# First half of the keys loaded as float32 through ScalarE's hardware queue, and cast on VectorE

## Chip, cores, metric

One core of a Trainium2 chip. The metric is the device time of one execution in microseconds (us). Most executions of a kernel agree within 0.3%, some 0.7 us here. In the views PE is TensorE, PEld its weight loads, DVE VectorE, ACT ScalarE, POOL GpSimd and SP SyncE. A hardware queue here is one that ScalarE or SyncE issues transfers on.

## The reference

Attention over 32 memory slots per head, then a bilinear feed-forward layer. The inputs are float32, the output is 4608 x 512 float32.

```python
# q, k, v: (8 batches, 8 heads, 576, 64); phi: (8, 8, 576, 32)
a = softmax(phi, axis=2)                      # over the sequence
k_m = einsum('bhsm,bhsd->bhmd', a, k)         # 32 keys per head
v_m = einsum('bhsm,bhsd->bhmd', a, v)
attn = softmax(q @ k_m.T / 8, axis=-1) @ v_m
x = attn -> (4608, 512)
out = ((x @ w_a) * (x @ w_b)) @ w_out         # w_a, w_b: 512x1536, w_out: 1536x512
```

## The kernel before

The kernel works in float16. Transfers issued by GpSimd cast from float32 on the way. phi alone stays float32 in SBUF, as ScalarE reads it for the exponential. All loads of the first two batches and all weights are issued ahead, in this order:

```python
kv_sbs = [consts.tile([P, 3, NHP, NI * D], F16, name=f"kv_sb{t}") for t in range(2)]

def load_phi(b):
    phis[b] = inp.tile([P, NHP, NI * M], F32, name="phi_sb")
    (nc.sync if b == 0 else nc.gpsimd).dma_start(out=phis[b], in_=rows(phi, b))

def load_k(b, hps=slice(0, NHP)):
    kvs[b] = kv_sbs[b % 2]
    nc.gpsimd.dma_start(out=kvs[b][:, 0, hps], in_=rows(k, b)[:, hps])
# ... load_v, load_q, load_wab (wa_sb and wb_sb), load_wo alike, on gpsimd

nc.scalar.preload_act_table_set("natural_log_exp_and_others")
load_phi(0)
halves = [slice(0, 2), slice(2, 4)]
for x in halves:
    load_k(0, x)
    load_q(0, x)
load_v(0)

warm = consts.tile([P, 512], F16, name="warm")
nc.vector.memset(warm, 0.0)
# ...
make_identity(nc, ident)
for t in range(2):
    nc.vector.memset(kv_sbs[t][:, 2], 1.0 / CS)      # the two masks
load_wab(0, 256)
# ... ones: a memset on vector, two affine_selects on gpsimd
load_wab(256, 512)
load_wab(512, 1024)
load_wab(1024, 1536)
load_wo(0)
load_phi(1)
load_k(1)
load_q(1, halves[0])
load_wo(1)
load_q(1, halves[1])
for x in halves:
    load_v(1, x)
load_wo(2)
```

The third plane of `kv_sb` is a constant mask; it makes the key sums (`ks`) also give the sum of the exponentials. The reciprocal of that sum and the scaling to `kvm` run on VectorE, then PE transposes.

```python
# sums(g, 0), called ks0 and ks1
for i in range(NI):
    for j in range(4):
        nc.tensor.matmul(pk[...], exp[..., i, :], kvs[b][..., part, hp, ...])   # cut
nc.vector.reciprocal(out=t["rphi"][:, g:g + 1], in_=pk[:, 1, 0:1])
nc.vector.tensor_scalar(out=t["kvm"][:, g, x], in0=pk[:, 0], scalar1=t["rphi"][:, g:g + 1], ...)
```

PE's order in the front is written out by hand. `fill(16)` and `f3` are warm-up matmuls on zeros, which stand where PE would be idle anyway. `hv0a` and so on fold `wa_sb` and `wb_sb` with the values (the `pva` matmuls), and `y2` does two output matmuls (`po`) of batch 0, which need the parts of `wo_sb` in turn:

```python
ht = consts.tile([P, NFF, 2 * S], F16, name="ht")     # the h ring, written only by the up stage

fill(16)
chain(0, "exp0 exp1 ks0 f3 kt0 qt0 qt1 f14 s0 e0 ks1 f3 kt1 qt2 qt3 f6 den0 ... hv0b hx0b f4")
# ... the up stage of batch 0, with the other folds beside it
chain(1, "exp0 exp1 y9 ks0 y3 kt0 ... vt0 vt1 nr1 y1 hv0a hx0a y2 hv0b hx0b y2")
```

The softmax here doesn't subtract the row's maximum and nothing guards it: scores larger than these inputs give would overflow.

Of the kernel before, what the change touches and what calls it, by code (L numbers as in the profile page):

```python
# [8 lines left out]
F32 = mybir.dt.float32  # L9
F16 = mybir.dt.float16  # L10
# [3 lines left out]
P = 128  # L14
CS = 16.0
# [3 lines left out]
def kernel(  # L19
# [11 lines left out]
    nc = tc.nc  # L31

    B, H, S, D = q.shape
# [4 lines left out]
    NFF = d_ff // P  # L38
# [4 lines left out]
    consts = ctx.enter_context(tc.tile_pool(name="consts", bufs=1))  # L43
# [26 lines left out]
    def rows(x, b):  # L70
        return x[b].rearrange("h s d -> (h s d)").rearrange("(c p f) -> p c f", c=NHP, p=P)

    phis, qs, kvs = {}, {}, {}
# [10 lines that stand above are left out]
    def load_v(b, hps=slice(0, NHP)):  # L84
        nc.gpsimd.dma_start(out=kvs[b][:, 1, hps], in_=rows(v, b)[:, hps])

    def load_q(b, hps=slice(0, NHP)):
        if b not in qs:
            qs[b] = inp.tile([P, NHP, NI * D], F16, name="q_sb")
        nc.gpsimd.dma_start(out=qs[b][:, hps], in_=rows(q, b)[:, hps])  # L90

    def load(b):
        load_phi(b)
        load_k(b)
        load_v(b)
        load_q(b)

    def load_wab(lo, hi):
        nc.gpsimd.dma_start(out=wa_sb[:, :, lo:hi], in_=wa_rows[:, :, lo:hi])
        nc.gpsimd.dma_start(out=wb_sb[:, :, lo:hi], in_=wb_rows[:, :, lo:hi])  # L100

    def load_wo(n):
        sl = slice(4 * n, 4 * (n + 1))
        nc.gpsimd.dma_start(out=wo_sb[:, sl, :], in_=wo_rows[:, sl, :])

    nc.scalar.preload_act_table_set("natural_log_exp_and_others")
    load_phi(0)
    halves = [slice(0, 2), slice(2, 4)]
    for x in halves:
        load_k(0, x)  # L110
        load_q(0, x)
    load_v(0)

    warm = consts.tile([P, 512], F16, name="warm")
    nc.vector.memset(warm, 0.0)
# [26 lines left out]
    def fill(n, cols=512):  # L142

        pw = banks.tile([P, 512], F32, name="pw")
        for _ in range(n):
            nc.tensor.matmul(pw[:, :cols], warm[:, :P], warm[:, :cols], start=True, stop=True)

    ident = consts.tile([P, P], F16, name="ident")
    make_identity(nc, ident)
    for t in range(2):  # L150
        nc.vector.memset(kv_sbs[t][:, 2], 1.0 / CS)
    load_wab(0, 256)

    ones = consts.tile([P, 4, 32], F16, name="ones")
# [2 lines left out]
                            pattern=[[-32, 4], [0, 32]], channel_multiplier=1)  # L157
    nc.gpsimd.affine_select(out=ones, in_=ones, compare_op=ALU.is_ge, fill=0.0, base=31,
                            pattern=[[32, 4], [0, 32]], channel_multiplier=-1)
    load_wab(256, 512)  # L160
    load_wab(512, 1024)
    load_wab(1024, 1536)
# [212 lines left out]
        u["-"] = lambda: None  # L375
        return u


    ht = consts.tile([P, NFF, 2 * S], F16, name="ht")
    out_rows = out.rearrange("(b p i) f -> b i p f", b=B, i=NI)  # L380

    def down_part(po, bank, cidx, lo, hi):
# [231 lines left out]
    def ups(steps, side=()):  # L614

        side = iter(side)
        for step in steps:
            for _ in up(*step):
                work.advance()
                next(side, us[step[0]]["-"])()  # L620
        for f in side:
            work.advance()
            f()

    def steps(b, lo, hi):

        return [(b, i, (0, 1)) for i in range(lo, hi)]
# [14 lines left out]
    def slots(b, names):  # L642

        def both(fs):
            return lambda: [f() for f in fs]
        def unit(n):
            if n == "fin":
                return lambda: work.pull(-work.done % NFF)
            if n == "L":
                return lambda: load(b + 2) if b + 2 < B else None  # L650
            if n[0] == "y":
                return lambda: some(int(n[1:]))
            if n[0] == "d" and n[1:].isdigit():
                return lambda: work.pull(int(n[1:]))
            return us[b + n.endswith("'") - n.endswith("_")][n.rstrip("'_")]

        return [both([unit(n) for n in x.split("+")]) for x in names.split()]
# [3 lines left out]
    def some(n):  # L661
        for _ in range(n):
            next(early, None)

    def chain(b, plan):


        for x in plan.split():
            if x[0] == "f":
                fill(int(x[1:]), 256)  # L670
            elif x[0] == "y":
                some(int(x[1:]))
            else:
                us[b][x]()
# [4 lines left out]
    ups(steps(0, 0, 4), slots(0, "- hv1a+hx1a - hv1b+hx1b - v1a+x1a - v1b+x1b"))  # L679
    load(2)  # L680
    ups(steps(0, 4, 12), slots(0, "- - - - v2a+x2a - v2b+x2b"))
    chain(1, "exp0 exp1 y9 ks0 y3 kt0 qt0 qt1 y1 ks1 y3 kt1 s0 e0 qt2 qt3 y6 den0 y2 s1 e1 nr0 y4 den1 y2 vs0 vs1 y1 vt0 vt1 nr1 y1 "
             "hv0a hx0a y2 hv0b hx0b y2")
    load(3)
    sum_weights()
    ups(steps(1, 0, 4), slots(1, "y1 hv1a+hx1a hv1b+hx1b y1 v1a+x1a v1b+x1b y3 y3"))
# [45 lines left out]
```

## Time and profile before

| | before |
|---|---|
| median of 3 runs (range) | 248.29 us (247.92 to 248.95) |
| PE busy, share of the span | 235.3 us, 95% |
| DMA engines full until | some 80 us, 13 of 40 slices |
| PE's last wait for a load in the front | 48.5 us, for the last part of `wo_sb` |

The front, up to 48.5 us, has more bytes to load than PE has work; after it PE sets the time. Two views are shown here. The first is the timeline of the kernel before; a line has start, duration, engine, line of the source, operation, tiles, shapes and, in brackets, the idle time of the engine before it and what ended it.

```profile
4.76 1.25 ACT L189 ACTIVATE exp_sb<-phi_sb 128x576 f16<-128x576 f32 x2 [2.67 <-DMA phi_sb<-in_phi_dram]
...
9.01 0.30 PE L268 MATMUL pT<-ident,kvm 128*32 128x128 f16 x8 [0.16 <-DVE kvm L260]
9.24 1.70 PE L146 MATMUL pw<-warm 128*128 128x256 f16 x14
```

phi is usable at 4.76; the first transposes start at 9.01. The second view has the windows of half a microsecond of the kernel before, with the busy time of PE, its weight loads, DVE, ACT and POOL, then the granted clock, the DMA share and the GB/s written.

```profile
2.50:3.00 0.50, 0.50 (x3) 0.21 (x2) 0.50 (x1) 0.00 (x0) 0.50 (x2) 1.00 0.78 242
3.00:3.50 0.50, 0.50 (x3) 0.23 (x2) 0.50 (x1) 0.00 (x0) 0.50 (x1) 1.00 1.08 389
```

The last column is how fast the DMA engines fill when phi is alone on a hardware queue. GpSimd's transfers take no part in it yet: issued from 1.32 us on, they have no packet in the trace before 3.8 us.

### The profile page before, as it was taken

To read this page: it belongs to the slowest core of one execution; us is meant where nothing else is said; L and a number is where in the kernel's file an instruction comes from. 1 tells how busy PE (TensorE), PEld (TensorE's weight loads), DVE (VectorE), ACT (ScalarE), POOL (GpSimd) and SP (SyncE) were. 2 spreads that over 40 slices of the span, in tenths; PEclk is the share of its full clock that TensorE was granted. 3 is DMA by queue.
4 is the path that set the end of the run, shared out by engine and by line. 5 is a ranking of instruction groups with operands and counts; after the bars stand their busy time and mean duration, and the time that the engine had idled before them with its cause. 6 is when DMAs were issued, how large, how long until landed. Compare 5 with 4: busy or idle time off the path is not lost.

```text
span 246.7 us, 7678 instructions
## 1 busy us (share of the span) xinstructions
PE 235.3 (95%) x3049; PEld 167.3 (68%) x3049; DVE 166.1 (67%) x400; ACT 158.1 (64%) x409; POOL 151.6 (61%) x124
## 2 busy tenths in 40 slices
PE   7989899999998999999999999999999999999992
PEld 2555464456655857777788777877787787888782
DVE  7247773477959967876994649865985676756620
ACT  4147761578697489578856768588855877465230
POOL 8834233499799029892889759892839186946000
PEclk9999999999999999999999999999999999999999
DMA  7999999999979804973159732695120303033145
GB/s 150 196 198 206 207 256 207 255 222 269 235 195 208 159 4 109 234 129 85 34 150 207 173 85 45 168 206 144 36 51 4 86 12 76 15 74 77 43 99 126
DMA packets 26036, 33.53 MB, mean 136 GB/s; under 512 B 1936, under 2 KB 20624, under 8 KB 26000
## 3 DMA queue, kind: packets, MB, share of 16 engines
q0 software_dynamic: 19552, 23.01, 51.2%
q1 hardware_dynamic: 6288, 9.90, 16.3%
q8 instruction: 24, 0.39, 0.6%
q10 hardware_dynamic: 160, 0.13, 0.2%
q14 instruction: 12, 0.10, 0.1%
HBM read 42.47 MB, written 9.44 MB: 210 GB/s over the span
## 4 chain that ended last, share of the span: by engine, by line
PE 74%; DMA 17%; DVE 3%; POOL 2%; issue 1%; ACT 1%; ACTq 0%; DVEq 0%; POOLq 0%
PE pa L598 18%; PE pb L608 16%; PE py L476 15%; PE pv L476 8%; DMA phi_sb<-in_phi_dram 6%; DMA wo_sb<-in_moe_w_out_dram 6%; PE pva L331 5%; DMA wb_sb<-in_moe_w_b_dram 5%; PE px L476 4%; PE po L385 3%; PE pkv L207 2%; PE pD L308 1%; PE pscore L286 1%; PE pT L236 1%; DVE A L319 1%
## 5 line engine op out<-in xcount | busy, mean ns | idle before, releaser
L611 DVE TENSOR_TENSOR ht<-a_sb,pb 128x288 f16<-128x288 f16 x192 | 82.9, 448 | 40.4 <-ACT a_sb L601 29.5
L601 ACT CAST a_sb<-pa 128x288 f16<-128x288 f32 x192 | 74.8, 405 | 31.3 <-PE pa L598 30.7
L598 PE MATMUL pa<-A,vab 128*128 128x288 f16 x384 | 76.6, 287 | 1.4 <-DVE A L319 1.4
L608 PE MATMUL pb<-A,vab 128*128 128x288 f16 x384 | 76.3, 286 | 0.2
L459 POOL TENSOR_TENSOR h_sums<-ht 128x768 f16<-128x768 f16 x28 | 45.8, 1638 | 34.0 <-DVE ht L611 34.0
L608 PEld LDWEIGHTS <-vab 128*128 128x128 f16 x384 | 37.0, 98 | 13.0 <-issue 1.9
L598 PEld LDWEIGHTS <-vab 128*128 128x128 f16 x384 | 34.5, 98 | 15.8 <-issue 9.1
L476 PEld LDWEIGHTS <-h_sums 128*128 128x128 f16 x360 | 35.1, 98 | 6.5 <-issue 0.4
L343 ACT CAST vab<-pva 128x512 f16<-128x512 f32 (+1 forms) x52 | 28.1, 558 | 11.8 <-PE pva L331 11.8
L343 DVE CAST vab<-pva 128x512 f16<-128x512 f32 (+1 forms) x52 | 32.8, 644 | 4.0 <-PE pva L331 3.6
L476 PEld LDWEIGHTS <-ht 128*128 128x128 f16 x270 | 26.4, 98 | 5.4 <-issue 0.2
L476 PE MATMUL py<-w_sums,h_sums 128*128 128x256 f16 x180 | 28.5, 272 | 0.0
L459 POOL TENSOR_TENSOR h_sums<-h_sums,ht 128x768 f16<-128x768 f16 x14 | 23.1, 1647 | 1.0
L459 POOL TENSOR_TENSOR h_sums<-ht,h_sums 128x768 f16<-128x768 f16 x14 | 23.0, 1640 | 1.0
L299 ACT ACTIVATE E<-pscore 128x288 f16<-128x288 f32 x32 | 11.4, 417 | 14.5 <-PE pscore L286 14.4
L319 POOL TENSOR_TENSOR A<-E,R 128x576 f16<-128x576 f16 x10 | 12.8, 1276 | 12.0 <-ACT R L317 11.7
L385 PE MATMUL po<-wo_sb,ht 128*128 128x512 f16 x60 | 16.0, 381 | 0.3 <-DMA wo_sb<-in_moe_w_out_dram 0.3
L476 PE MATMUL py<-wo_sb,ht 128*128 128x256 f16 x90 | 15.2, 273 | 0.0
L476 PE MATMUL pv<-w_sums,h_sums 128*128 128x256 f16 x90 | 15.2, 273 | 0.0
L198 DVE STREAM_TRANSPOSE qT<-q_sb 128x288 f32<-128x288 f32 x32 | 14.5, 463 | 1.0 <-DMA q_sb<-in_q_dram 1.0
L476 PE MATMUL py<-w_sums,ht 128*128 128x256 f16 x90 | 14.7, 272 | 0.1
L476 PE MATMUL px<-wo_sb,ht 128*128 128x256 f16 x90 | 14.6, 273 | 0.0
(64 smaller groups left out, 271.2 us busy)
## 6 DMA issues: line engine op xcount, KB each, us to landing
out_dram<-o_sb SPq DMA_DIRECT2D x70, 128.0 KB, 2.4
kv_sb<-in_v_dram POOLq DMA_DIRECT2D x7, 576.0 KB, 10.0
phi_sb<-in_phi_dram POOLq DMA_DIRECT2D x7, 576.0 KB, 4.6
kv_sb<-in_k_dram POOLq DMA_DIRECT2D x7, 576.0 KB, 8.8
q_sb<-in_q_dram POOLq DMA_DIRECT2D x6, 576.0 KB, 12.7
wo_sb<-in_moe_w_out_dram POOLq DMA_DIRECT2D x3, 512.0 KB, 16.6
q_sb<-in_q_dram POOLq DMA_DIRECT2D x4, 288.0 KB, 12.6
wa_sb<-in_moe_w_a_dram POOLq DMA_DIRECT2D x2, 512.0 KB, 14.9
```

The source lines that it names most:

```text
L198: nc.vector.transpose(out=t["qT"][:, hp, :].bitcast(F32), in_=qs[b][:, hp, :].bitcast(F32))
L299: nc.scalar.activation(out=Ev[:, g, :, z, :], in_=pss, func=AF.Exp, scale=1.0 / (8.0 * CS))
L319: engine.tensor_tensor(out=attn[b][:, g, sl], in0=t["E"][:, g, sl], in1=t["R", g][:, sl], op=ALU.mult)
L331: nc.tensor.matmul(t["pva", lo, z][g][0][32 * j:32 * j + 32, 0:hi - lo], t["kvT"][64 * r:64 * r + 64, 4 + g, M * j:M * j + M], w_sbs[z][64 ...
L343: engine_copy(out=vabs[b][z][:, g, lo:hi], in_=pva[:, 0:hi - lo])
L385: nc.tensor.matmul(po, ht[:, i, P * c:P * (c + 1)], wo_sb[:, i, :], start=(i == 0), stop=(i == NFF - 1))
L459: engine.tensor_tensor(out=out, in0=in0, in1=in1, op=op)
L476: nc.tensor.matmul(po, lhs[:, i], rhs[:, i], start=first and i == 0, stop=i == KH - 1, skip_group_check=not first)
L598: nc.tensor.matmul(pa, vab[0][:, g, fs], A[:, g, HALF * hf:HALF * (hf + 1)], start=(g == 0), stop=(g == 1))
L601: nc.scalar.copy(out=a_sb, in_=pa)
L608: nc.tensor.matmul(pb, vab[1][:, g, fs], A[:, g, HALF * hf:HALF * (hf + 1)], start=(g == 0), stop=(g == 1))
L611: nc.vector.tensor_tensor(out=ht[:, i, t0:t0 + HALF], in0=a_sbs[hf - hfs[0]], in1=pb, op=ALU.mult)
```

## The change

The intent: GpSimd's queue is where all loads are issued one after the other. Taking its first transfer away and giving it to ScalarE's idle hardware queue lets every later load be issued one place earlier. A transfer from a hardware queue does not cast (the prediction names the page that says so), so the keys land as float32 in the part of the h ring that nothing needs yet, and VectorE casts them into place. To have VectorE free for the cast, the mask of the other buffer moves behind it. The small memset of `ones` comes to stand behind the cast too.

```diff
+    ht = consts.tile([P, NFF, 2 * S], F16, name="ht")
+    k_f32 = ht[:, 0:2].bitcast(F32)
+    nc.scalar.dma_start(out=k_f32, in_=rows(k, 0)[:, 0:2])
     nc.scalar.preload_act_table_set("natural_log_exp_and_others")
     load_phi(0)
     halves = [slice(0, 2), slice(2, 4)]
-    for x in halves:
-        load_k(0, x)
-        load_q(0, x)
+    load_q(0, halves[0])
+    load_k(0, halves[1])
+    load_q(0, halves[1])
     load_v(0)
+    kvs[0] = kv_sbs[0]
...
-    for t in range(2):
-        nc.vector.memset(kv_sbs[t][:, 2], 1.0 / CS)
+    nc.vector.memset(kv_sbs[0][:, 2], 1.0 / CS)
+    nc.vector.tensor_copy(out=kvs[0][:, 0, 0:2], in_=k_f32)
     load_wab(0, 256)
...  (ones)
+    nc.vector.memset(kv_sbs[1][:, 2], 1.0 / CS)
     load_wab(256, 512)
...
-    ht = consts.tile([P, NFF, 2 * S], F16, name="ht")   (its old place)
```

More of the change, by code (lines that the diff above doesn't have):

```diff
@@ L376, in units @@
         return u
-    ht = consts.tile([P, NFF, 2 * S], F16, name="ht")
     out_rows = out.rearrange("(b p i) f -> b i p f", b=B, i=NI)
@@ L681 @@
     ups(steps(0, 4, 12), slots(0, "- - - - v2a+x2a - v2b+x2b"))
-    chain(1, "exp0 exp1 y9 ks0 y3 kt0 qt0 qt1 y1 ks1 y3 kt1 s0 e0 qt2 qt3 y6 den0 y2 s1 e1 nr0 y4 den1 y2 vs0 vs1 y1 vt0 vt1 nr1 y1 "
-             "hv0a hx0a y2 hv0b hx0b y2")
+    chain(1, "exp0 exp1 y9 ks0 y3 kt0 qt0 qt1 y1 ks1 y3 kt1 s0 e0 qt2 qt3 y6 den0 y2 s1 e1 nr0 y4 den1 y2 vs0 vs1 y1 vt0 vt1 nr1 y1 hv0a hx0a y2 hv0b hx0b y2")
     load(3)
```

## The prediction

> **What bounds the kernel now.** The page comes first: PE is busy 95% of the span at an undisturbed clock, every other engine below 70%. So the end is set by PE's in-order stream, and a change is worth what it takes out of PE's gaps. The slices show where these can be: the DMA engines are full for the first thirteen of forty slices, some 80 us, and then drop.
>
> ```profile
> PE 235.3 (95%) x3049; PEld 167.3 (68%) x3049; DVE 166.1 (67%) x400; ACT 158.1 (64%) x409; POOL 151.6 (61%) x124
> DMA  7999999999979804973159732695120303033145
> ```
>
> The chain that ended last, in order of time, shows the front as a relay of loads:
>
> ```profile
> 6.41 11.38 DMA wb_sb<-in_moe_w_b_dram
> 17.79 0.28 issue
> 18.07 15.67 DMA phi_sb<-in_phi_dram
> 33.74 14.75 DMA wo_sb<-in_moe_w_out_dram
> 48.49 0.04 issue
> 48.54 0.59 PE po L385 x2
> ```
>
> Each landing frees a slot from which GpSimd issues the next, but seven or eight transfers are always in flight, so what is short is transfer rate. After 48.5 us the chain is PE alone. What PE waited for in the first 60 us says how tightly the loads hold it:
>
> ```profile
> PE pva L331 <- DMA wb_sb<-in_moe_w_b_dram: 1.6, 2, 1.1
> PE po L385 <- DMA wo_sb<-in_moe_w_out_dram: 0.3, 1, 0.3
> ```
>
> Keys and queries are not in this list. The timeline of the first microseconds tells why:
>
> ```profile
> 1.26 6.54 PE L146 MATMUL pw<-warm 128*128 128x512 f16 x16 [1.26 <-DVE warm L115]
> 1.32 0.89 POOL L82 DMA_DIRECT2D kv_sb<-in_k_dram  x1 [0.80 <-POOLq L716]
> ...
> 4.04 1.98 DVE L151 MEMSET kv_sb<- 128x2304 f16 x1 [0.43 <-issue]
> ...
> 7.73 0.68 PE L250 MATMUL pk<-kv_sb,exp_sb 64*32 64x128 f16 x36
> ...
> 8.47 0.17 DVE L259 RECIPROCAL rphi<-pk 128x1 f32<-128x1 f32 x1 [2.31 <-PE pk L250]
> ```
>
> The sixteen warm-up matmuls run at 427 ns each (their weight loads are 0.43 us apart) until 7.80 us, and the first key sums follow without a gap. The first half of the keys, issued at 1.32, had landed 5.7 us later (the shortest of the three key transfers in the tile view), at 7.0 us. So the first key sums wait for the warm-up in front of them, not for the keys. And DVE sat idle 2.31 us ahead of the reciprocal: its two mask memsets were over by 6.02 us.
>
> **What the Trainium skill says.** "DMA: Bandwidth & Descriptors", section "Issuing engines are not separate DMA queues": transfers issued from ScalarE, SyncE or GpSimd end on the same 16 DMA engines and interleave; spreading the issue saves only sequencer time. The trace agrees: once full, the loads write 205 to 207 GB/s of float16, hence read some 410 GB/s of float32, and a second queue cannot add to that. The same page, "SWDGE vs HWDGE vs iDMA": a transfer that casts has to be issued by GpSimd; hence the float32 landing and a cast on VectorE. "VectorE: DVE Perf Modes", "Mode 2×_2P": a copy with a single source in SBUF can use both read ports and do two float32 elements per cycle. The trace before has no such copy. "SBUF — State Buffer", "SBUF: two separate sides": during such a copy GpSimd is locked out and cannot write descriptors. No line before shows that either.
>
> **The change part by part.**
>
> *Removed:* one transfer at the head of GpSimd's queue. It took 0.89 us, the following ones 0.72 us, so every later load is issued about 0.72 to 0.88 us earlier. By itself this yields little, as from 4 us on the queue is never empty.
>
> *Added, transfer:* 576 KB on ScalarE's queue at about 0.8 us, in the place of the table load, which moves back by an issue (0.45 us for phi on SyncE) and still ends near 2.6 us, before phi lands. The HBM bytes are the same; only the write side doubles. The gain is that the DMA engines fill sooner. In the windows of half a microsecond they moved 14, 83 and 242 GB/s in 1.5 to 3.0 us, then 389. With two hardware transfers from 1.5 us on I assume double the first two and about 390 for the third: (14 + 83 + 148) GB/s x 0.5 us = 0.12 MB, or 0.3 us at 410 GB/s. From 4.5 to 6.5 us they wrote only 154 to 168 GB/s (some 330 read); if float32 keys hold 390 for the first 1 to 1.5 us of that, another 0.06 to 0.09 MB, 0.2 us. Sum: all later landings **0.5 us earlier**, my estimate, between 0.2 and 0.9.
>
> *Added, cast:* 128x1152 elements. The nearest rows are the casts from PSUM, 421 ns for 256 and 685 ns for 512 elements, 1.03 ns an element, hence 1.3 us at one element per cycle; at two, about 0.7 us. I choose 0.7. phi and keys share the engines: 1.18 MB at 390 GB/s is 3.0 us from a start near 2 us, plus about half a microsecond to confirm, so both land near 5.6 us (phi before: 4.7). exp0 would then be ready by 6.3 us, the cast by 6.3 to 6.9, both before the warm-up ends at 7.80. ks0 does not move.
>
> *Moved:* the second mask memset, 1.98 us, now stands behind cast and ones (0.17) and ahead of the first reciprocal. It runs from about 6.8 to 8.8, or 9.2 with the 0.43 us pause seen before memsets. The reciprocal was at 8.47, so the first transposes, scores and all of batch 0's chain start **0.3 to 0.8 us later**. This eats DVE idle time first (2.31 us of it), then PE time.
>
> *What reaches the end:* PE's first two waits for weights absorb the delay. In front of the second-chunk fold at 25.59 PE stood 0.47 us, in front of the last one 1.08:
>
> ```profile
> 25.59 0.41 PE L331 MATMUL pva<-wb_sb,kvT 64*32 64x512 f16 x8 [0.47 <-DMA wb_sb<-in_moe_w_b_dram]
> 31.36 0.41 PE L331 MATMUL pva<-wb_sb,kvT 64*32 64x512 f16 x8 [1.08 <-DMA wb_sb<-in_moe_w_b_dram]
> ```
>
> With a delay of 0.8 us PE reaches the first 0.33 us late, and the last at 31.36 - 1.08 + 0.33 = 30.6, where the weights land at 31.36 - 0.5 = 30.9. So PE still waits there and leaves 0.5 us earlier than before: the landing, not the early chain, passes its shift on. The wait for wo_sb at 48.5 moves by the same 0.5. Behind that PE is busy 69.55 of 70 us (80 to 150), so the shift is carried to the end. Sum: 248.29 - 0.5 = **247.8 us**.
>
> **The rivals.** (1) *The early chain becomes the bound.* If float32 keys land at 7 us or the cast runs at one element per cycle, the reciprocal comes at 10 us or later, 1.5 us behind; then 1.0 us is left at the first wait, PE is at the last fold at 31.3 and nothing is gained: 248.2 to 248.6. For it: three streams share the engines, and memset and cast are in strict order. Against it: 1.55 us of waits have to be used up first. (2) *The transfers gain nothing*, as the bytes are the same and doubled writes cost as much as the earlier start brings: 248.3. For it: the engines' share is over 1 from 3.0 us. (3) *The whole issue shift counts*, 0.9 us, because the start-up is latency and not rate: 247.4. Against it: the queues were already backed up from 4 us. (4) *The cast locks GpSimd out*: 0.7 us of issue with four or five transfers queued; no effect.
>
> **Range and chances.** The times before spread from 247.92 to 248.95, so 0.5 us is near the noise. A gain of 1.0 us is the most the loads can yield, a loss of 0.4 the worst of the early chain, with some noise on both: 247.1 to 248.7. Two per cent are 5 us; no part here is worth a third of that, so within 2% is all but certain.
>
> **What would show it.** Right: ks0 starts at 7.7 to 7.8 us still; the reciprocal after it comes later than 8.47, with DVE in the second mask memset until then; the last wb_sb fold starts near 30.9 with a smaller wait for its DMA; the po matmul waiting for wo_sb is near 48.0; the PE sum is unchanged. Wrong: if ks0 begins past 8 us (keys late), if no DMA wait is left at the last fold (the early chain bounds), if the landings have not moved, or if a PE wait arises after 50 us.

## The result, and the profile after

| | before | after |
|---|---|---|
| median, us (range, 4 runs each) | 248.27 (247.92 to 248.95) | 247.98 (247.87 to 248.15) |
| ratio of means, 95% interval | | 0.9986 (0.9963 to 1.0008) |
| first reciprocal | 8.47 | 9.94 |
| last `wb_sb` fold starts, PE idle before it | 31.36, 1.08 | 31.45, none |
| `po` for the last part of `wo_sb` starts | 48.54 | 48.43 |
| span of the profiled run | 246.7 | 246.4 |

A ratio is the mean time of one kernel's runs over that of the other's of the same rounds, so it is not quite the ratio of the medians. The interval includes 1: these rounds do not separate the two kernels. The result is correct.

The line of PE on the page of the kernel after is as good as unchanged, as the change neither adds nor removes work there:

```profile
PE 234.4 (95%) x3049; PEld 167.1 (68%) x3049; DVE 166.5 (68%) x401; ACT 157.9 (64%) x409; POOL 151.1 (61%) x123
```

The timeline after, in the lines that answer to those of before:

```profile
0.81 0.50 ACTq L109 DMA_DIRECT2D ht<-in_k_dram  x1
1.26 5.54 PE L151 MATMUL pw<-warm 128*128 128x512 f16 x16 [1.26 <-DVE warm L120]
...
6.71 0.76 DVE L156 CAST kv_sb<-ht 128x1152 f16<-128x1152 f32 x1 [3.10 <-DMA ht<-in_k_dram]
7.08 1.26 ACT L195 ACTIVATE exp_sb<-phi_sb 128x576 f16<-128x576 f32 x2 [4.45 <-DMA phi_sb<-in_phi_dram]
7.82 0.68 PE L256 MATMUL pk<-kv_sb,exp_sb 64*32 64x128 f16 x36 [1.02 <-ACT exp_sb L195]
8.04 1.98 DVE L165 MEMSET kv_sb<- 128x2304 f16 x1 [0.43 <-issue]
9.94 0.10 DVE L265 RECIPROCAL rphi<-pk 128x1 f32<-128x1 f32 x1
...
10.41 0.30 PE L274 MATMUL pT<-ident,kvm 128*32 128x128 f16 x8 [1.48 <-DVE kvm L266]
...
31.45 0.41 PE L337 MATMUL pva<-wb_sb,kvT 64*32 64x512 f16 x8
...
48.43 0.59 PE L389 MATMUL po<-wo_sb,ht 128*128 128x512 f16 x2
```

Read it from the top. The keys were cast at 6.71. phi, which ran alone on its queue before and released ACT at 4.76, now released it only at 7.08. The first key sums waited 1.02 us for the exponential of phi. The moved mask ran from 8.04 to 10.02, and the reciprocal, which needs only 0.1 us and stands behind it, started at 9.94, 1.47 us later than before. The fold at 31.45 has no bracket: PE came to it with no wait left. And yet the `po` at 48.43 is 0.11 earlier.

What PE waited for in the first 60 us of the kernel after (total, times, longest) has no weight left in it:

```profile
PE pT L274 <- DVE kvm L266: 1.9, 3, 1.5
PE pk L256 <- ACT exp_sb L195: 1.0, 1, 1.0
```

The chain of the kernel after (start, duration, what) has the same relay of loads as before, 0.3 us ahead at its last hand-over and 0.1 us at its end:

```profile
5.69 12.22 DMA wb_sb<-in_moe_w_b_dram
18.19 15.25 DMA phi_sb<-in_phi_dram
33.44 14.95 DMA wo_sb<-in_moe_w_out_dram
```

The first hand-over went from 6.41 to 5.69, the full issue shift of 0.72 us. It is not simply carried on: the second came at 18.19, 0.12 us later than before (18.07), the third was 0.30 us ahead, and the last landing 0.1 us. One reason why the issue shift could not last is on GpSimd:

```profile
7.69 0.31 POOL L161 TENSOR_SCALAR_AFFINE_SELECT ones<-ones 128x128 f16<-128x128 f16 x1 [1.25 <-DVE ones L160]
```

GpSimd waited 1.25 us for `ones`, that is for the cast and so for the keys, and issued the next load at 8.33 us, where the kernel before had issued it at 7.82. (It waits so in all eleven traces with the cast, 0.88 to 1.40 us, and no run takes this wait away.) The bytes show no harm from it: by my estimate, twice the bytes written less those that were float32, the lead over the kernel before grew from 0.08 MB at 7 us to 0.17 MB at 10 us, as earlier transfers were still in flight. But the later loads were not issued earlier, as the change had meant them to be. For the start of the transfers, the half-microsecond windows after, columns as before:

```profile
2.50:3.00 0.50, 0.50 (x3) 0.21 (x2) 0.50 (x1) 0.14 (x1) 0.50 (x2) 1.00 0.70 177
3.00:3.50 0.50, 0.50 (x3) 0.23 (x2) 0.50 (x1) 0.00 (x0) 0.50 (x1) 1.00 0.69 214
```

With two hardware transfers started together the DMA engines moved 177 and 214 GB/s where they had moved 242 and 389. By 6 us no more had been read than before (1.17 against 1.21 MB by the same estimate), so the faster fill that the change was to bring did not come.

Two gates can be seen then: the *last fold* at 31.4 us and the *last part of `wo_sb`* at 48.4 us. To follow a delay through the kernel, the matmuls of two traces were matched one to one. After against before: +0.09 us at the first key sums, +1.4 at the first transposes, +1.6 at the first value sums, +1.05 at the second-chunk fold, +0.09 at the last one, -0.11 at the `po`, and about -0.1 from there to the end. The traces thus explain 0.1 us of the 0.3 between the medians.

### The profile page after: what moved, and what is told of

It reads as the page before. It is cut to its first block, busy times and chain, and to the rows that moved or that the text cites. A ratio compares the mean times of both kernels' runs of the same rounds, so it can differ in the third digit from the quotient of the medians.

```text
span 246.4 us, 7681 instructions
## 1 busy us (share of the span) xinstructions
PE 234.4 (95%) x3049; PEld 167.1 (68%) x3049; DVE 166.5 (68%) x401; ACT 157.9 (64%) x409; POOL 151.1 (61%) x123
## 4 chain that ended last, share of the span: by engine, by line
PE 74%; DMA 17%; DVE 3%; POOL 2%; ACT 1%; issue 1%; ACTq 0%; DVEq 0%; POOLq 0%
PE pa L602 18%; PE pb L612 16%; PE py L480 15%; PE pv L480 8%; DMA phi_sb<-in_phi_dram 6%; DMA wo_sb<-in_moe_w_out_dram 6%; DMA wb_sb<-in_moe_w_b_dram 5%; PE pva L337 5%; PE px L480 4%; PE po L389 3%; PE pkv L213 2%; PE pD L314 1%; PE pscore L292 1%; PE pT L242 1%; POOL q_sb L90 1%
## 5 line engine op out<-in xcount | busy, mean ns | idle before, releaser
L325 POOL TENSOR_TENSOR A<-E,R 128x576 f16<-128x576 f16 x10 | 12.8, 1278 | 11.9 <-ACT R L323 11.6
L315 ACT ACTIVATE L<-pD 128x288 f32<-128x288 f32 x32 | 11.4, 413 | 5.0 <-PE pD L314 4.8
```

The costliest lines, as they stand in the source:

```text
L325: engine.tensor_tensor(out=attn[b][:, g, sl], in0=t["E"][:, g, sl], in1=t["R", g][:, sl], op=ALU.mult)
```

## The experiments

Twelve runs in four calls, each call on another chip. Each has its own runs of the kernel before, with medians of 248.31 (first: e1, e2, c1, f1), 248.59 (second: g1, g4, c3, f2) and 248.83 us (third: h1 to h3); the ratios are against those. The table has all runs, in us; "last landing" is the end of the transfer of the last part of `wo_sb`.

| run | median (range) | ratio (95%) | first reciprocal | last fold, wait | last landing | `po` |
|---|---|---|---|---|---|---|
| e1_mask_early | 248.08 (247.79–248.65) | 0.9994 (0.9974–1.0013) | 8.56 | 30.68, 0.35 | 48.4 | 48.42 |
| e2_keys_behind_phi | 248.01 (247.29–248.55) | 0.9986 (0.9966–1.0006) | 9.95 | 31.45, none | 47.8 | 48.23 |
| c1_before_late | 249.57 (249.00–250.68) | 1.0054 (1.0032–1.0076) | 11.00 | 33.23, none | 48.6 | 50.01 |
| f1_pad_before_wo2 | 249.70 (249.38–250.90) | 1.0060 (1.0038–1.0082) | 9.87 | 31.44, none | 49.7 | 49.76 |
| g1_both | 247.58 (246.89–247.86) | 0.9956 (0.9942–0.9970) | 8.39 | 30.18, none | 47.8 | 47.78 |
| g4_both_late_po | 247.16 (246.95–247.69) | 0.9948 (0.9935–0.9961) | 7.90 | 30.58, 0.92 | 47.7 | 47.72 |
| c3_before_late16 | 248.78 (248.43–249.08) | 1.0009 (0.9997–1.0020) | 9.81 | 31.05, none | 48.8 | 48.81 |
| f2_pad_after_wo2 | 248.20 (248.16–248.69) | 0.9989 (0.9977–1.0001) | 9.86 | 31.45, none | 47.8 | 48.23 |
| h1_keys_after_table | 248.67 (one look) | – | 9.93 | 31.44, none | 48.3 | 48.28 |
| h2_after_again | 248.00 (247.65–248.70) | 0.9966 (0.9949–0.9983) | 9.85 | 31.43, none | 48.3 | 48.28 |
| h3_best_again | 247.07 (246.91–247.28) | 0.9928 (0.9914–0.9941) | 8.29 | 30.17, 0.35 | 47.8 | 47.84 |
| h4_keys_late | 248.68 (one look) | – | 10.09 | 32.32, none | 48.1 | 49.09 |

The theory at the start: the late mask delays batch 0's chain, this eats the wait at the last fold, and the landing of the last part of `wo_sb` sets the end all the same, so that the small gain is that landing's. Its rival: the early chain is the bound now, and giving the mask its old place brings time. A second question was where the 0.5 us of earlier landings went.

### e1_mask_early: the second mask back in its old place

```diff
     nc.vector.memset(kv_sbs[0][:, 2], 1.0 / CS)
+    nc.vector.memset(kv_sbs[1][:, 2], 1.0 / CS)
     nc.vector.tensor_copy(out=kvs[0][:, 0, 0:2], in_=k_f32)
...
-    nc.vector.memset(kv_sbs[1][:, 2], 1.0 / CS)
```

> The changed kernel with one thing undone: the second mask memset goes back ahead of the cast, into the 3.1 us in which VectorE waits for the keys. Theory A (the landing of the last wo_sb part at 48.4 us sets when PE leaves the front; the late reciprocal was absorbed by waits for weights): the first reciprocal moves from 9.94 to about 8.6 us, the first transposes from 10.41 to about 9.1, PE waits again 0.3 to 0.8 us for the last wb_sb part near 31 us, and the po matmul at 48.43 stays within 0.1 us, so the time stays at that of the changed kernel, 247.9 to 248.1 us. Rival B (the late reciprocal is what ate the gain at the end): po comes 0.3 us or more earlier and the time falls by 0.3 us or more.

Measured: 248.08 us, ratio to before 0.9994, so not apart from the kernel after (0.9986). The timeline of this run:

```profile
8.56 0.17 DVE L265 RECIPROCAL rphi<-pk 128x1 f32<-128x1 f32 x1 [0.94 <-PE pk L256]
...
30.68 0.41 PE L337 MATMUL pva<-wb_sb,kvT 64*32 64x512 f16 x8 [0.35 <-DMA wb_sb<-in_moe_w_b_dram]
...
48.42 0.59 PE L389 MATMUL po<-wo_sb,ht 128*128 128x512 f16 x2
```

The reciprocal is back at 8.56, the wait at the last fold is back with 0.35 us, and this fold starts 0.77 us earlier than in the kernel after. At the `po` nothing of this is left: 48.42 against 48.43. So the late mask was the cause of the late chain and took what the last fold could have gained; and the second gate made that worth nothing.

### e2_keys_behind_phi: the keys issued by SyncE, behind phi

```diff
-    nc.scalar.dma_start(out=k_f32, in_=rows(k, 0)[:, 0:2])
     nc.scalar.preload_act_table_set("natural_log_exp_and_others")
     load_phi(0)
+    nc.sync.dma_start(out=k_f32, in_=rows(k, 0)[:, 0:2])
```

> The changed kernel, but the float32 keys are issued by SyncE behind phi, on the same queue. Theory A (three rings share the 16 engines, so phi, with the smallest packets, was held up to 7.05 us by the keys): phi lands at 4.8 to 5.5 us, the keys at 6.5 to 7.0, the first key sums start when the cast ends, near 7.6; the end does not move (within 0.2 us of the changed kernel), as the sum of bytes ahead of the last wo_sb part is the same. Rival (the hardware queues are slow however they are split): phi lands past 6 us also here.

Measured: 248.01 us, ratio 0.9986. The timeline of this run for phi and keys:

```profile
5.17 1.26 ACT L195 ACTIVATE exp_sb<-phi_sb 128x576 f16<-128x576 f32 x2 [3.08 <-DMA phi_sb<-in_phi_dram]
...
6.73 0.76 DVE L156 CAST kv_sb<-ht 128x1152 f16<-128x1152 f32 x1 [3.12 <-DMA ht<-in_k_dram]
```

And its windows:

```profile
2.50:3.00 0.50, 0.50 (x3) 0.21 (x2) 0.50 (x1) 0.00 (x0) 0.50 (x2) 1.00 0.74 228
3.00:3.50 0.50, 0.50 (x3) 0.22 (x2) 0.50 (x1) 0.00 (x0) 0.50 (x1) 1.00 1.08 329
```

phi releases ACT at 5.17 in place of 7.08, and the keys are no later than with their own queue (6.73, 6.71). The engines fill faster again. By 8 us about 0.13 MB more had been read than in the kernel after (my estimate, twice the bytes written less those that were float32: 2.19 against 2.06 MB), which is 0.3 us at 410 GB/s. The last landing was at 47.8 instead of 48.4 (but f2, below, without this edit, had 47.8 too). The mask was still late here, PE came to the `po` only at 48.23 with no wait, and so only 0.20 us of it was used. This asks for both edits in one kernel (g1, below).

### c1_before_late: the kernel before, with its chain delayed

Two more mask memsets on VectorE in the kernel before; its transfers are untouched.

```diff
+    for _ in range(2):
+        nc.vector.memset(kv_sbs[1][:, 2], 1.0 / CS)
     load_wab(256, 512)
```

> The kernel before, with two more memsets of the same mask on VectorE ahead of the first reciprocal: no transfer changes, the reciprocal moves from 8.47 to about 10.1 us (1.6 us later). Theory A (the waits for weights absorb up to 0.47 + 1.08 us of a delay in batch 0's chain): PE's two waits for wb_sb vanish, po at 48.5 is at most 0.1 us later and the time rises by 0 to 0.2 us. Rival B: the time rises by more than 0.8 us.

Measured: 249.57 us, ratio 1.0054. I had mis-sized this run: there were pauses of 0.43 and 0.55 us ahead of the two memsets, and the reciprocal came at 11.00, 2.5 us late. Then something came on top. The timeline of PE in this run, and below it one of its windows:

```profile
11.49 0.30 PE L270 MATMUL pT<-ident,kvm 128*32 128x128 f16 x8 [2.57 <-DVE kvm L262]
11.71 3.05 PE L146 MATMUL pw<-warm 128*128 128x256 f16 x14
```

```profile
12.00:13.00 1.00, 1.00 (x6) 0.73 (x5) 0.87 (x3) 0.00 (x0) 0.74 (x1) 0.50 1.22 210
```

The fourteen warm-up matmuls that took 1.70 us before took 3.05 here, and the granted clock (third number from the end) was 0.50 from 11.9 to 15.3 us. PE had been idle 1.06 us before the key sums and 2.57 us before the transposes; behind that the array ran at half speed for some 3.4 us. The delay grew to 4.05 us, was +1.87 at the last fold and +1.47 at the `po`, and stayed to the end. So the run shows that a delay of the early chain that outgrows the waits does reach the end; as a copy of the change's delay it was too large. c3 repeats it in the right size.

### c3_before_late16: the same with the delay in the size of the change

```diff
+    nc.vector.memset(kv_sbs[1][:, 2], 1.0 / CS)
+    nc.vector.memset(kv_sbs[1][:, 2, 0:2], 1.0 / CS)
     load_wab(256, 512)
```

> The kernel before with one and a half more memsets ahead of the first reciprocal, sized so that this comes at about 10.1 us, 1.6 us late, as in the changed kernel (two whole ones came to 11.0, and left PE idle 2.6 us, behind which the warm-up matmuls ran at half speed again). Theory A: the first transposes at 10.5, no slow matmuls, the waits for wb_sb gone, the last wb_sb fold near 31.4 (0 to 0.1 us late), po within 0.1 us of 48.54, time within 0.2 us of the kernel before. Rival B: time up by 1 us or more.

Measured: 248.78 us, ratio 1.0009 (0.9997 to 1.0020), with the reciprocal at 9.81 (9.94 in the kernel after). The timeline of PE:

```profile
31.05 0.41 PE L333 MATMUL pva<-wb_sb,kvT 64*32 64x512 f16 x8
...
48.81 0.59 PE L387 MATMUL po<-wo_sb,ht 128*128 128x512 f16 x2
```

The wait at the last fold is gone here as well, the fold is no later than in the kernel before (31.05 against 31.36), and the `po` starts with its load, which landed at 48.8 in this execution (48.5 in the kernel before, whose transfers are the same). The forecast of the `po` (within 0.1 us of 48.54) was missed by this landing. A delay of this size costs nothing measurable alone: the weight waits absorb it.

### f1_pad_before_wo2 and f2_pad_after_wo2: bytes before and behind the last gate

A load of 576 KB of float32 into a part of the h ring that is overwritten before it is read (the results stay correct), issued just before or just after the last part of `wo_sb`.

```diff
+    nc.gpsimd.dma_start(out=ht[:, 10:12, S:2 * S], in_=rows(q, 2)[:, 0:2])   # f1
     load_wo(2)
+    nc.gpsimd.dma_start(out=ht[:, 10:12, S:2 * S], in_=rows(q, 2)[:, 0:2])   # f2
```

> The changed kernel with one useless load of 288 KB of float16 (590 KB read) into a part of the h ring that is still idle, put in GpSimd's queue directly ahead of the last wo_sb part. Theory A (bytes in front of the last wo_sb part set the front): po moves from 48.43 by 1.2 to 1.5 us (590 KB at 410 GB/s is 1.44 us, 0.14 us of slack) and the time rises by 1.1 to 1.5 us. Rival B (PE's own work bounds the front): less than 0.5 us.

> The changed kernel with the same useless load as in the run with it ahead of the last wo_sb part, but directly behind that part. Theory A (only bytes ahead of that part hold PE): po stays within 0.2 us of 48.43 and the time within 0.3 us of the changed kernel, against 1.7 us more with the load ahead. Rival (any added load costs its bytes): 1.2 us or more.

Measured: f1 249.70 us, ratio 1.0060; f2 248.20 us, ratio 0.9989. Against the ratio of the kernel after, 0.9986, f1 costs 0.74% or 1.8 us (more than the 1.1 to 1.5 expected, and less sharp than it looks, as both intervals are some 0.2% to either side) and f2 nothing. The timeline of f1:

```profile
49.76 0.59 PE L390 MATMUL po<-wo_sb,ht 128*128 128x512 f16 x2 [1.47 <-DMA wo_sb<-in_moe_w_out_dram]
```

The `po` moved by 1.33 us, close to the 1.44 us that 590 KB take at 410 GB/s. So bytes ahead of the last part of `wo_sb` are paid nearly one to one, and the same bytes behind it are free. (In f2's trace the lead over the kernel before falls from 0.29 us at the `po` to 0.09 at 61 us, behind a wait of 0.17 us for VectorE; whether the added load has to do with it is open.) This shows that this landing can hold the front's end. In the kernel after it held it by little: where the load had landed early (47.8 in e2 and f2), PE came to the `po` at 48.23 with no wait, only 0.20 us before 48.43.

### g1_both: mask early, and keys behind phi

The edits of e1 and e2 together.

> The keys behind phi on SyncE's queue and the second mask memset back ahead of the cast: both repairs at once. In the run with the keys behind phi, the last wo_sb part landed near 47.8 us (issued 33.0, 14.8 to landing) and PE, not it, was late (48.23). Theory A: with the mask early, the reciprocal is at 8.3 us, PE reaches the last wb_sb fold early and waits there, leaves by 30.3, and po starts when wo_sb lands, 47.8 to 48.0; the time is 0.1 to 0.3 us below the run with the keys behind phi alone and 0.5 to 0.7 below the kernel before: 247.6 to 247.8. Rival (no gain is left in the front): as the changed kernel.

Measured: 247.58 us, ratio 0.9956 (0.9942 to 0.9970), that is 1.1 us faster than before (expected 0.5 to 0.7). The wait at the last fold that was expected did not show. The timeline of PE:

```profile
47.78 0.59 PE L389 MATMUL po<-wo_sb,ht 128*128 128x512 f16 x2 [0.49 <-DMA wo_sb<-in_moe_w_out_dram]
48.30 0.30 PE L337 MATMUL pva<-wb_sb,kvT 64*32 64x256 f16 x8
```

e1 brought PE early to a late landing, e2 brought the landing early to a late PE; with both, the `po` starts at 47.78, where e1 had 48.42, e2 48.23 and the kernel after 48.43. In time, the intervals of g1 and of the kernel after still overlap a little, and they are from different rounds; the trace carries this step, and h3 below settles it for the version that follows. Now PE stands 0.49 us in front of it again, while a fold that needs only weights long landed comes behind it.

### g4_both_late_po: the fold before the po

```diff
-... nr1 y1 hv0a hx0a y2 hv0b hx0b y2
+... nr1 y1 hv0a hx0a hv0b hx0b y4
```

> As the run with both repairs, and in the tail of batch 1's chain the four po matmuls that need the last wo_sb part come behind both wb folds instead of two of them between. Theory A (PE waits for that part with a fold of 0.24 us ready behind it): up to 0.25 us less wait, time 0 to 0.25 us below the run with both repairs. Rival: ScalarE's and VectorE's copies of the folds then open a gap in PE of 0.3 us or more, and the time rises by as much.

Measured: 247.16 us, ratio 0.9948 (0.9935 to 0.9961). The timeline of PE:

```profile
47.17 0.37 PE L337 MATMUL pva<-wb_sb,kvT 64*32 64x256 f16 x8
47.72 1.02 PE L389 MATMUL po<-wo_sb,ht 128*128 128x512 f16 x4 [0.18 <-DMA wo_sb<-in_moe_w_out_dram]
```

The fold now fills the wait, of which 0.18 us is left, and matched matmuls are 1.15 us ahead of the kernel before from here on (0.76 in g1). The gain on g1 was 0.4 us in both the trace and the medians, a little over the 0.25 expected. The intervals of g1 and g4 overlap, so the step from one to the other is shown by the trace but not by the clock.

### h1_keys_after_table, h2_after_again, h3_best_again

h1 moves ScalarE's issue behind the table load, to have the keys start later on the same queue. h2 is the kernel after, h3 is g4, both unchanged.

```diff
-    nc.scalar.dma_start(out=k_f32, in_=rows(k, 0)[:, 0:2])
     nc.scalar.preload_act_table_set("natural_log_exp_and_others")
+    nc.scalar.dma_start(out=k_f32, in_=rows(k, 0)[:, 0:2])     # h1
```

> The changed kernel with the float32 keys still on ScalarE's own queue, but issued behind the activation table's load, near 2.1 us and not 0.81. It tells apart why phi and keys together filled slowly (177 and 214 GB/s from 2.5 to 3.5 us against 228 and 329 with both on SyncE's queue, and phi at 7.05 against 5.17 us). Theory C (phi shares the engines by ring, in step with the keys, from its first packet): phi, with a head start of 1.3 us, lands by 5.6 us and the windows from 2.5 to 3.5 us are at 230 GB/s or more; the keys land at 7 us or later. Rival D (a second hardware queue in itself slows the first): phi still lands past 6.3 us. Time not judged (one look).

> The changed kernel itself again, beside the best one, to have both against the kernel before in the same rounds and to see how much of its trace repeats: reciprocal at 9.9, no wait for wb_sb, po at 48.2 to 48.5, ratio 0.998 to 1.000. The end of the warm-up matmuls may lie anywhere from 6.6 to 7.8 us.

> The kernel with both repairs and the late po matmuls again: if its gain is real, ratio 0.993 to 0.997 again, 1.0 to 1.4 us below the kernel before and 0.7 to 1.1 below the changed kernel of the same rounds; po near 47.7 us.

Measured: h1 did not do what it was for. The issue stayed at 0.84 us, beside the table load, and phi released ACT at 7.08 again with 118 and 173 GB/s in the two windows; it is a repeat of the slow fill and no test of its cause. h2: 248.00 us, ratio 0.9966 (0.9949 to 0.9983); on this chip the kernel after is faster than the one before by 0.3%, some 0.8 us, where the first rounds left 0.3 us in doubt. That is below the ratio of 0.998 to 1.000 expected, and the trace of h2 shows only 0.25 us of it (matched matmuls, from the `po` to the end); there is no trace of the kernel before on this chip. h3: 247.07 us, ratio 0.9928 (0.9914 to 0.9941). The best version was ahead of the kernel before both times, on two chips, by 1.3 and 1.8 us (the traces have 1.15 and 1.04 us), and in the rounds that h2 and h3 share the two intervals are apart: it beats the kernel after as well.

### h4_keys_late: the issue on ScalarE held back by a memset

```diff
-    nc.scalar.dma_start(out=k_f32, in_=rows(k, 0)[:, 0:2])
...
     nc.vector.memset(warm, 0.0)
+    nc.vector.memset(ht[:, 0, 0:2], 0.0)
+    nc.scalar.dma_start(out=k_f32, in_=rows(k, 0)[:, 0:2])
```

> The run with the keys behind the table load failed to delay them (the issue went out at 0.84 us beside the table load). Here a memset of two elements of the h ring, behind the one of the warm-up tile on VectorE, holds the issue on ScalarE's queue until about 1.7 us, 0.9 us behind phi. Theory C (phi is held up because the keys share the engines with it from the first packet): phi lands by 5.6 us. Rival D (a second hardware queue in itself slows the first): phi lands past 6.3 us. The keys land at 6.6 us or later in both. Time not judged (one look).

Measured: the issue came at 1.26 us (planned 1.7), 0.45 us later than in the kernel after. Its time is not judged. Its timeline for phi and keys:

```profile
5.31 1.25 ACT L196 ACTIVATE exp_sb<-phi_sb 128x576 f16<-128x576 f32 x2 [3.22 <-DMA phi_sb<-in_phi_dram]
...
6.86 0.76 DVE L157 CAST kv_sb<-ht 128x1152 f16<-128x1152 f32 x1 [3.24 <-DMA ht<-in_k_dram]
```

phi is back at 5.31, though the keys are on ScalarE's queue as in the change, and the windows show 251 and 283 GB/s. So it is not the second queue in itself that held phi back, but that the keys moved at the same time. The DMA queues of the traces show how. From 3.75 to 5.25 us the kernel after moved 171 packets (0.38 MB) of the keys and 185 (0.21 MB) of phi: nearly packet for packet, but the keys' packets are twice as large, so phi got about a third of the bytes. From 2.0 to 3.5 us phi had moved 0.16 MB there, and 0.36 MB in h4, where the keys had no packet yet. Why the engines moved so little in all from 2.5 to 3.5 us in the kernel after, when the keys had few packets yet (39 by 3.5 us), I could not settle. The run had the half clock too: PE was idle 1.41 and 1.77 us before the key sums and the transposes, and the same fourteen warm-up matmuls took 3.09 us.

## Why the prediction was right or wrong

The time was right: 247.8 us predicted, 247.98 measured, in the range of 247.1 to 248.7. Part of that is luck: the two largest steps, the early landings and the wait that remains at the last fold, were wrong, and both the forecast and the measured gain are within the noise of the first rounds.

- **"ks0 does not move": the number right, the reason wrong.** It started at 7.82. But the step said that it waits for the warm-up. After, the warm-up ended at 6.80, and PE stood 1.02 us for the exponential of phi. The end of the warm-up is not fixed: over the fourteen traces it lies between 6.27 and 7.80, and the kernel before happened to have the latest. The sixteen matmuls start 427 ns apart at first and 216 ns apart later, and in these traces the step between the two came anywhere from 4.1 us (h4) to 7.2 us (before). That 7.08 plus one exponential fell on the old start is chance. The same reading of one trace, that keys are not waited for, does not hold in general: in c1 PE waited 1.06 us for the keys of the unchanged transfers, in c3 0.26 us.
- **"both land near 5.6 us": wrong.** The keys were there at 6.71, phi at 7.08. The term that failed is the assumed 390 GB/s from 2.5 us on; the windows have 177 and 214. e2 and h4 show that the keys starting somewhat later brings phi to 5.17 and 5.31 at almost no cost to the keys (6.73 and 6.86).
- **The cast: right.** 0.7 us chosen, 0.76 measured, where the sum for one element per cycle gave 1.3.
- **The reciprocal "0.3 to 0.8 us later": mis-sized.** It was 1.47. The cast was ready at 7.47 instead of at most 6.9, the pause of 0.43 us ahead of the memset, which the prediction had only as the worse case, was there, and the memset took its 1.98 us: together 2.41 us, which is also the distance between the starts of the two masks in e1 (1.63 and 4.04).
- **The last fold "still waits and leaves 0.5 us earlier": wrong.** No wait was left, which the prediction had named as a sign of being wrong, and it started 0.09 us later than before. This is the mechanism of rival 1 with nearly its arithmetic (reciprocal at 10 us, the fold at 31.3 with nothing gained). e1 shows that the mask's order is the cause: with it undone the fold starts at 30.68.
- **Landings "0.5 us earlier": right in sign, too large.** The last hand-over of the chain moved by 0.30, the last landing by 0.1 to 0.2 us. That "every later load is issued about 0.72 to 0.88 us earlier" held for the first six of GpSimd's loads only. The seventh came 0.51 us later than before, as GpSimd waited for `ones` behind the cast, a wait that the prediction did not see. And its early fill (0.12 MB ahead by 3.0 us) did not come.
- **"The wait for wo_sb at 48.5 moves by the same" and is carried to the end: right in kind, by 0.1 and not 0.5 us.** f1 and f2 show that bytes ahead of this load are paid and bytes behind it are not. The last fold lost its gain, but PE had 0.33 us of waiting at the `po`, 17 us further on, and this took up the 0.09 us. So the time stayed below rival 1's price of 248.2 to 248.6. This second gate, which the prediction named only in passing, is what it should have started from.
- **Rival 2** (nothing gained, 248.3) came close in what the bytes do. The first rounds do not exclude it, the repeat in h2 does (0.9966). **Rival 3** (the whole issue shift counts) did not come: the shift was gone at the second hand-over. **Rival 4** (the cast locks GpSimd out) is open: GpSimd issued nothing during the cast, as it was waiting for `ones` behind it, so no run shows it.

What stays open is the exact size of the landings' shift. The last part of `wo_sb` landed at 48.3 to 48.4 in the kernel after, h1, h2 and e1, but at 47.8 in f2, which has the same transfers ahead of it and ran on another chip than e1, h1 and h2. With the keys behind phi it landed at 47.7 to 47.8 in all four traces (e2, g1, g4, h3). That the best version is faster is measured twice; how much of its earlier landing is due to phi's start, these traces do not settle. On the chip of g1 and g4 the one trace with the change's own order of transfers is f2's, and there it landed as early as in g1 and g4.

## What to carry to other kernels

When loads pace the front, find the last load that PE waits for and ask of each edit whether it moves that landing and whether PE is there in time: here each half alone gave nothing that could be measured, and both together, with one fold moved in front of the wait, gave 1.3 to 1.8 us against the kernel before. When an operation is moved behind another on an engine that works in order, work out when what it now stands in front of becomes ready; a memset of 2 us before a reciprocal of 0.1 us cost a gate its whole slack. Look also at what stands behind the operation on other engines: here GpSimd's issue of loads came to wait for a cast on VectorE. And do not read from one trace that something is never waited for when what hides it is a warm-up whose end varies from run to run.

## What the Trainium skill lacked or had wrong

- "DMA: Bandwidth & Descriptors", "Issuing engines are not separate DMA queues": that such transfers interleave holds (171 and 185 packets in the same 1.5 us), but the page has no figure for what two hardware transfers that start together do to each other. Here phi released its reader at 7.08 us when started with the keys, and at 5.17 (e2) or 5.31 (h4) when the keys started a little later; the fill was 177 and 214 GB/s against 228 and 329, or 251 and 283.
- "TensorE: Matmul & The Clock Gate", "HAM oscillation — how this bites in real kernels": it gives the rule "no PE-idle gaps >~3.4µs". Its next section tells of shorter idle times that do the same in another kernel, without their length. Here two gaps of 1.06 and 2.57 us (c1), or of 1.41 and 1.77 us (h4), were followed by a granted clock of 0.50 and fourteen matmuls in 3.05 and 3.09 us instead of 1.70. Gaps of 1.02 and 1.48 us (after) and of 0.64 and 1.77 us (e2) were not. So the length of the longest gap does not decide it; what does, these traces do not show. In the first microseconds the matmuls took 427 ns for 512 columns, while the column of the granted clock said 1.00: in the warm-up only the durations tell.
- "VectorE: DVE Perf Modes", "Zero memsets can be issued as uint32 (trn2)": the page gives a memset one cycle per element, which at its 0.96 GHz makes an estimate of 2.40 us for 2304 elements. The record of the mask's memset shows only 1.98 us, with 0.43 us of idle time before it; the sum is 2.41. So the page agrees with the distance of the starts in e1 (c1 has one of 2.53) and not with the recorded duration, which the page doesn't say: whoever adds up durations, as the prediction did in its better case, comes out 0.43 us short. For the cast, the section "Side-by-side: where the cycles go for N=2048 bf16" agrees: about 150 cycles, 8 to fill the pipe, and 576 for 1152 elements at two per cycle, make an estimate of 765 ns, where 759 ns was measured.
- No page has it that the landing of the same transfers differs by some 0.5 us between executions (48.3 in h2, 47.8 in f2, on two chips).
